# A planned attention, expert and feed-forward kernel on one core: the last slots' chain without fillers, fewer dummy transposes, one copy per half unit of y, and the carried phase row scaled by GpSimd

## The chip, the cores and the metric

The kernel runs on one core of a Trainium2 chip. The metric is the device time of one execution in microseconds (us). Three timed runs of the kernel before are at hand, and one more execution that the hardware profiler took.

## What is computed

Three stages follow each other, all in float32.

```python
# 1: gated linear recurrence, B=4, H=8, S=768, D=48
mag = np.sqrt(a_re * a_re + a_im * a_im)
scale = np.minimum(mag, 0.999) / (mag + 1e-06)
...
for t in range(S):
    new_re = ar * S_re - ai * S_im
    new_im = ar * S_im + ai * S_re
    kv = np.einsum('bhd,bhe->bhde', k[:, :, t], v[:, :, t])
    S_re, S_im = (new_re + kv, new_im)
    y[:, :, t] = np.einsum('bhd,bhde->bhe', q[:, :, t], S_re)
...
# 2: soft mixture of experts: x is y as 3072 tokens x 384; phi 384 x 32 slots
logits = x @ phi
d = softmax of logits over the tokens, c = softmax over the slots
slot_input = d.T @ x                     # 32 slots x 384
h = np.maximum(slot_input[e] @ w1[e], 0.0)   # 8 experts, 4 slots each, 384 x 1024
slot_out[e] = h @ w2[e]
x = c @ slot_out
# 3: feed-forward, 384 x 2048 x 384
h = x @ w_in
out = np.maximum(0.01 * h, h) @ w_out
```

## The kernel before, in words

The program is not written in the order in which it runs. Every step is handed to a `Plan` as an operation with an engine, a guessed cost, the tiles it reads and the tiles it writes. `emit` computes a due time for each by a pass from the end (`backward`), lets a pass from the start (`forward`) pick for each engine the next operation by earliest start and due time, repeats this six times and writes out the best order. A `lead` makes an operation due that many us earlier. An operation of VectorE (DVE) or ScalarE (ACT) that is due `FAR` us or more later than the most pressing one is a filler: it is picked only when half of its cost would fit. Tiles come from tagged pools with a fixed number of buffers (33 of the large tag `w`), and a step whose buffer is still in use waits.

**Units.** Stage 1 is cut into 12 units: 6 chunks of 128 time steps by 2 halves of the 32 sequences. A unit is a tile of 128 steps by 768 columns (16 sequences of 48). Its steps and their lines: `load_a`, `load_qkv` (L493, L352); `prep1` (L515 to L518) logarithm, exponent and ratio; `prep2` arctangent (L554), and from the third unit on the phase carried over from two units before, added into row 0 by a DMA that GpSimd (POOL) issues (L557); `phase`: running sums over the steps as a product with a triangle (PE L570), rounded by ACT (L581) and DVE (L582), absolute value (L583), and the last row times a constant for the unit after next (L586, on 32 partitions by 768); `prep3` sine and cosine (L593, L594); `decay` the sums of the logarithms and their exponents (L606, L607), whose last row goes through DRAM into a small tile (L611, L613). `prep4` multiplies q and k with them (L623, L632). `attend` is the unit's TensorE (PE) work: transposes (L647, copied by L653 and L651), scores (L662, masked by L665), y (L688), state update (L703, L713 to L716); `mE` copies y out (L724), transposes it (L728), and copies it out again in two pieces of 192 columns (L732).

Unit 0 is cut into pieces of 192, 192 and 384 columns, so that the chain at the start is short. `warm` (L823) issues transposes of the identity that compute nothing, 150 at the start and 20 after the last logits.

**Slots.** After each second unit `slots` takes the logits of 512 tokens (L748), a running maximum (L752, L754, L755), the exponent (L756), transposes (L762, L763), the slots' sums (L771, accumulated by L777) and the denominator (L778, L779). After the last chunk a product with ones brings the four groups to one maximum (L899 to L904); `si_t` adds the groups up (L911, copied by L914).

**Experts.** 64 slabs of weights of 384 KB come in over the whole program, by the queue of SyncE (SP), as buffers come free. `layer1(gr)` (L932, ReLU by ACT L937 and DVE L939, transposes L943, copies L950) and `layer2(gr)` (L968, L975, L979, L987) each run for two groups of experts. `combine` is the softmax over the slots, its transposes are L880.

**Feed-forward.** `product` multiplies the experts' output with w_in (L1005, L1008, L1009) and spreads the result (L1013, L1014, copied by L1018 and L1020). `ffn1` (L1030, then L1032 to L1034) and `ffn2` (L1047 to L1049) run over 16 chunks of the inner dimension for 8 groups of 384 tokens. w_in and w_out arrive as 64-bit words and are narrowed by `conv_wi` and `conv_wo` (L445 on ACT, L446 to L449 on DVE, and for w_out L477 and L478). These conversions are the fillers.

## Time and profile before

| | us |
|---|---|
| three timed runs | 514.16, 513.96, 512.84 (median 513.96) |
| the profiled execution | 512.59 |
| its span | 510.7 |
| PE busy | 491.8 (96%) |
| ACT busy | 357.4 (70%) |
| DVE busy | 330.4 (65%) |
| POOL busy | 13.0 (3%) |
| DMA moved | 66.98 MB |

The shares are means over stages that differ. The units run from the start to about 245, the last slots to 251, the experts and the product to 284, the feed-forward to the end. A busy PE is one with matmuls in flight, not one at its peak. In the rows "<-" behind an idle time names what ended it.

### The profile page before, as it was taken

The numbers are of one execution on the slowest core, as the hardware profiler recorded it, in microseconds if no ns is written. First come the engines' busy times: TensorE is split into PE (matmuls) and PEld (weight loads), VectorE is DVE, ScalarE is ACT, GpSimd is POOL, SyncE is SP. The second block draws the span as 40 slices with busy tenths as digits, with TensorE's granted clock in tenths as the row PEclk, the third lists the DMA queues.
The fourth block names the chain that finished last, engine by engine and source line by source line (L and its number), as shares of the span: only waits on it lengthen the run. The fifth ranks groups of instructions, "written<-read, shape, count | busy, mean of one in ns | idle before, by whom it ended". The sixth has DMA issues, their size and how long they took to land.

```text
span 510.7 us, 10607 instructions
## 1 busy us (share of the span) xinstructions
PE 491.8 (96%) x4155; PEld 447.9 (88%) x4155; DVE 330.4 (65%) x705; ACT 357.4 (70%) x702; POOL 13.0 (3%) x27
## 2 busy tenths in 40 slices
PE   8987989999999999999899999999999999999997
PEld 8785869888889888889654899999999999999997
DVE  3588999999999998997534999415500552035300
ACT  7799999999989999864204899249900993079502
POOL 1000000000000000001000000000000000000000
PEclk9999999999999999999999999999999999999999
DMA  7956253473443856679899321011000110010102
GB/s 261 361 193 186 73 174 130 99 206 104 154 127 126 247 171 235 195 242 335 287 361 399 104 62 32 2 37 42 15 1 0 47 48 1 1 46 2 47 0 92
DMA packets 43845, 66.98 MB, mean 131 GB/s; under 512 B 19098, under 2 KB 24970, under 8 KB 43796
## 3 DMA queue, kind: packets, MB, share of 16 engines
q1 hardware_dynamic: 43476, 66.29, 39.2%
q8 instruction: 32, 0.52, 0.4%
q0 software_dynamic: 320, 0.03, 0.1%
q14 instruction: 17, 0.14, 0.1%
HBM read 61.53 MB, written 4.75 MB: 130 GB/s over the span
## 4 chain that ended last, share of the span: by engine, by line
PE 68%; DVE 17%; ACT 8%; DMA 3%; issue 2%; POOL 0%; SPq 0%; POOLq 0%; ACTq 0%; DVEq 0%
PE b L1047 13%; PE b L1048 13%; PE b L1049 13%; PE b L1030 4%; PE bm L823 4%; PE bm L688 3%; PE bsc L662 3%; PE btr L647 3%; DVE sc L665 2%; PE b L932 2%; PE b L968 2%; DVE k L632 2%; DVE q L632 2%; PE bsc L703 2%; PE bc L570 2%
## 5 line engine op out<-in xcount | busy, mean ns | idle before, releaser
L1034 DVE TENSOR_TENSOR w<-x,w 128x384 fp32r<-128x384 f32 x128 | 67.8, 555 | 105.9 <-ACT w L1033 105.9
L1047 PE MATMUL b<-w 128*128 128x384 f32 x384 | 128.6, 335 | 0.8 <-ACT x L1032 0.8
L1048 PE MATMUL b<-w 128*128 128x384 f32 x384 | 128.6, 335 | 0.0
L1049 PE MATMUL b<-w 128*128 128x384 f32 x384 | 128.3, 334 | 0.0
L1047 PEld LDWEIGHTS b<-w 128*128 128x128 f32 x384 | 72.1, 188 | 1.0 <-ACT x L1032 1.0
L1049 PEld LDWEIGHTS b<-w 128*128 128x128 f32 x384 | 72.1, 188 | 0.0
L1048 PEld LDWEIGHTS b<-w 128*128 128x128 f32 x384 | 72.1, 188 | 0.0
L1056 ACT ACTIVATE k<-b 128x384 f32<-128x384 f32 x24 | 11.3, 487 | 82.5 <-PE b L1049 82.3
L1033 ACT ACTIVATE w<-x 128x384 fp32r<-128x384 f32 x128 | 62.9, 531 | 6.1 <-PE b L1049 5.0
L1032 ACT ACTIVATE x<-b 128x384 f32<-128x384 f32 x128 | 58.7, 494 | 3.8 <-PE b L1030 3.1
L662 PE MATMUL bsc<-qt,kt 96*128 96x128 f32 x384 | 51.8, 280 | 1.9 <-DVE S L715 0.8
L662 PEld LDWEIGHTS bsc<-qt,kt 96*128 96x128 f32 x384 | 46.2, 191 | 5.4 <-issue 1.9
L688 PE MATMUL bm<-sc,w 128*64 128x128 f32 (+1 forms) x384 | 36.4, 277 | 0.1
L665 DVE TENSOR_TENSOR sc<-bsc,tri_r 128x512 f32<-128x512 f32 x48 | 32.5, 682 | 3.1 <-PE bsc L662 2.9
L647 PE MATMUL btr<-ident,q 128*96 128x128 f32 x192 | 29.5, 276 | 3.8 <-ACT qt L653 2.3
L186 ACT ACT_TABLE_LOAD x25 | 32.1, 1283 | 1.2 <-PEq L1141 0.8
L703 PEld LDWEIGHTS bsc<-w,k 128*96 128x96 f32 x320 | 29.0, 165 | 3.4 <-DVE sc L665 2.5
L703 PE MATMUL bsc<-w,k 128*96 128x48 f32 x320 | 30.3, 247 | 1.6 <-DVE sc L665 1.5
L688 PE MATMUL bm<-qt,S 96*48 96x128 f32 x320 | 31.2, 272 | 0.0
L653 ACT ACTIVATE qt<-btr 96x512 f32<-96x512 f32 x48 | 28.2, 589 | 3.6 <-PE btr L647 3.5
L647 PE MATMUL btr<-ident,k 128*96 128x128 f32 x192 | 29.0, 274 | 1.3 <-ACT w L525 0.7
L647 PEld LDWEIGHTS btr<-ident,q 128*96 128x96 f32 x192 | 20.8, 127 | 8.4 <-ACT qt L653 3.3
(177 smaller groups left out, 822.8 us busy)
## 6 DMA issues: line engine op xcount, KB each, us to landing
w<-in_w_dram SPq DMA_DIRECT2D x49, 384.0 KB, 6.5
w<-in_qkv_dram SPq DMA_DIRECT2D x36, 384.0 KB, 6.0
w<-in_a_dram SPq DMA_DIRECT2D x22, 384.0 KB, 4.5
w<-in_wi_dram SPq DMA_DIRECT2D x16, 384.0 KB, 4.7
w<-in_wo_dram SPq DMA_DIRECT2D x16, 384.0 KB, 5.6
out_dram<-k SPq DMA_DIRECT2D x24, 192.0 KB, 1.9
cs<-in_w_dram SPq DMA_DIRECT2D x6, 384.0 KB, 5.0
k<-in_w_dram SPq DMA_DIRECT2D x6, 192.0 KB, 6.2
```

Of the source, the lines that this page charges most:

```text
L186: self.preload(TABLES[name])
L647: T.transpose(b()[:96, P * i:P * i + P], src()[:, i].rearrange("p t d -> p (t d)"), ident)
L662: T.matmul(b()[:, P * i:P * i + P], lhsT=k()[:96, i, :], rhs=q()[:96, i, :], start=True, stop=True)
L665: dve(c_dve(512), lambda: V.tensor_tensor(t(), b().rearrange("p (i t) -> p i t", t=P), tri.unsqueeze(1).to_broadcast([P, 4, P]), op=ALU.mu ...
L688: T.matmul(y()[64 * j:64 * j + m, o:o + P], lhsT=l, rhs=r, start=kind == 0, stop=kind == 1 or c == 0)
L703: T.matmul(b()[:96, D * i:D * i + D], lhsT=ks[i // 4]()[:, i % 4].rearrange("p t d -> p (t d)"), rhs=v()[:, D * g:D * g + D], start=True, ...
L1032: act(NG, lambda: A.activation(u(), b()[:, :NG], AF.Prelu, alpha=0.01), [b], [u])
L1033: act(NG, lambda: A.activation(g()[:, 0], u(), AF.Copy), [u], [(g, 0)])
L1034: dve(c_dve(NG), lambda: V.tensor_tensor(g()[:, 1], u(), g()[:, 0].bitcast(F32), op=ALU.subtract), [u, (g, 0)], [(g, 1)])
L1047: T.matmul(b()[:, :DM], lhsT=lh, rhs=wh()[:, i], start=f == FO[0], stop=False)
L1048: T.matmul(b()[:, :DM], lhsT=ll, rhs=wh()[:, i], start=False, stop=False)
L1049: T.matmul(b()[:, :DM], lhsT=lh, rhs=wl()[:, i], start=False, stop=f == FO[-1])
```

## The change

In words, with the lines of the changed kernel where they are new:

- The real and imaginary parts of unit 0 are loaded by two queues, SP's and ACT's; phi is loaded later, in the place of unit 0 in the plan.
- 100 dummy transposes at the start in place of 150, 14 in place of 20 at the end; their guessed cost is 0.16 in place of 0.11.
- In `phase` the rounded phase stays in the tile `im` (L582, L583); the last row is no longer scaled by DVE. It is written to DRAM (L589), read back as a tile of 128 x 6 (L590), scaled by POOL (L591) and written to DRAM again (L592), from where POOL's accumulating DMA takes it (L558).
- In `mE` one copy of 384 columns (L737) takes the place of the two.
- In `slots` the running minimum of the negated maximum is kept, so that one DVE operation goes; the exponent's own accumulator gives the row sum, so that the reduction goes. The accumulation of the last chunk is cut in three, and so is `si_t`.
- `FAR` is 10 in place of 20. The last chunk's slots, `si_t`, the end of `layer2(1)`, `product`, the first `conv_wo` and the first `ffn1` get leads of 25 or 26. `select` waits for the slots' sums.

```diff
-NEAR, FAR = 0.03, 20.0
+NEAR, FAR = 0.03, 10.0
...
-    SY.dma_start(phi, r_in)
...
+                far = u == 0 and i
+                plan.add("ACT" if far else "SP", 0.1, lambda b=b, i=i, o=o, e=e, far=far: (A if far else SY).dma_start(b()[:, o:e], a_in[u, i][:, o:e]), [], [(b, o)], nbytes=P * (e - o) * 4)
...
-            plan.add("POOL", 1.0, lambda: GP.dma_start(im()[0:1, :], cr()[127:128, :], accum_op=ALU.add), [cr], [(im, o) for o, _ in cuts(u)], nbytes=3072)
+            plan.add("POOL", 1.0, lambda: GP.dma_start(im()[0:1, :], cr().unsqueeze(0), accum_op=ALU.add), [cr], [(im, o) for o, _ in cuts(u)], nbytes=3072)
...
-            cr = s["cr"] = t_w()
-            dve(c_dve2(W), lambda: V.tensor_scalar(cr()[96:128], cs()[96:128, 1], -TWO_PI, None, op0=ALU.mult), [(cs, 1, o) for o, _ in cu], [cr])
+            row = t_dr()
+            cr = t_cr()
+            carried = s["cr"] = t_dr()
+            plan.add("SP", 0, lambda: SY.dma_start(row().unsqueeze(0), im()[P - 1:P, :]), [(im, o) for o, _ in cu], [row], nbytes=3072)
+            plan.add("SP", 0, lambda: SY.dma_start(cr(), row().rearrange("(p f) -> p f", p=P)), [row], [cr], nbytes=3072)
+            pool(0.12, lambda: GP.tensor_scalar(cr(), cr(), -TWO_PI, 0.0, op0=ALU.mult, op1=ALU.add), [], [cr])
+            plan.add("SP", 0, lambda: SY.dma_start(carried().rearrange("(p f) -> p f", p=P), cr()), [cr], [carried], nbytes=3072)
...
-        for j in range(2):
-            act(192, lambda j=j: A.activation(
-                x().rearrange("p (r j e) -> p r j e", j=2, e=D)[:, :, j, :],
-                b()[:, 0:448].rearrange("p (r w) -> p r w", w=112)[:, :, 64 * j:64 * j + D], AF.Copy), [b], [(x, j)])
+        act(384, lambda: A.activation(
+            x().rearrange("p (r j e) -> p r j e", j=2, e=D),
+            b()[:, 0:512].rearrange("p (r w) -> p r w", w=128)[:, :, 0:2 * 64].rearrange("p r (j w) -> p r j w", w=64)[:, :, :, 0:D], AF.Copy), [b], [(x, 0), (x, 1)])
...
+        plan.lead = 25.0 if last else 0.0
...
-            dve(0.07, lambda: V.tensor_tensor(m1, m1, m0, op=ALU.max), [("mx", c)], [("mx", c + 1)])
-        dve(0.07, lambda: V.tensor_scalar(n1, m1, -1.0, None, op0=ALU.mult), [("mx", c + 1)], [("nm", c + 1)])
+            dve(0.07, lambda: V.tensor_scalar(n1, m1, -1.0, n0, op0=ALU.mult, op1=ALU.min), [("mx", c + 1), ("nm", c)], [("nm", c + 1)])
...
-            dve(0.2, lambda: V.tensor_reduce(sm1(), e(), axis=AX.X, op=ALU.add), [e], [sm])
...
-    warm(150, b_m)
+    warm(100, b_m)
...
-    warm(20, b_c, [phi_mm])
+    warm(14, b_c, [phi_mm])
...
+    plan.lead = 25.0
     product()
     for f in FO[:4]:
+        plan.lead = 26.0 if f in FO[:1] else 0.0
         conv_wo(f)
```

The order changes in many places. Three of them follow. The first is PE's order at the start, up to the first transposes of unit 0: L570 (L571 after) are the sums for the decay (`tri_r`) and for the phase (`tri_p`), L823 (L832 after) the dummies. Before:

```order
L823 MATMUL bm<-ident 128x128 x78
L570 MATMUL bsc<-w,tri_r 128x192 x6
L823 MATMUL bm<-ident 128x128 x8
L570 MATMUL bm<-w,tri_r 128x384 x3
L823 MATMUL bm<-ident 128x128 x49
L570 MATMUL btr<-w,tri_p 128x192 x2
```

and after:

```order
L832 MATMUL bm<-ident 128x128 x53
L571 MATMUL bsc<-w,tri_r 128x192 x3
L832 MATMUL bm<-ident 128x128
L571 MATMUL bsc<-w,tri_r 128x192 x3
L832 MATMUL bm<-ident 128x128 x5
L571 MATMUL bm<-w,tri_r 128x384 x3
L832 MATMUL bm<-ident 128x128 x34
L571 MATMUL btr<-w,tri_p 128x192 x2
```

Ahead of the decay stand 53 dummies where 78 stood, and between decay and phase 34 where 49 stood.

The second is DVE's order around the last chunk's maximum (L752, L758 after), up to the product with the identity that the common maximum starts with (L899, L910 after). L876 (L887 after) belongs to the softmax over the slots, L800 and L804 (L809 and L813 after) to `select`. Before:

```order
L876 TENSOR_TENSOR kt<-logits,kt 128x3x64
L804 CAST sc<-stk 32x2x32
L800 TENSOR_SCALAR sc<-stk 128x512
L804 CAST sc<-stk 32x2x32
L752 TENSOR_REDUCE mx<-bsc 128x1
L804 CAST sc<-stk 32x2x32
L754 TENSOR_TENSOR mx<-mx 128x1
L804 CAST sc<-stk 32x2x32
L755 TENSOR_SCALAR nm<-mx 128x1
L804 CAST sc<-stk 32x2x32
L899 TENSOR_SCALAR kt<-ident,mx 128x128
```

and after:

```order
L887 TENSOR_TENSOR kt<-logits,kt 128x3x64 x3
L758 TENSOR_REDUCE mx<-bsc 128x1
L760 TENSOR_SCALAR nm<-mx,nm 128x1
L769 COPY dd<-bsc 128x128
L910 TENSOR_SCALAR kt<-ident,nm 128x128
```

`select` has moved behind the chain (it follows L923).

The third is SP's queue at the experts' last slabs. Before:

```order
L352 DMA qt<-in_w_dram 128x384 x2
L352 DMA x<-in_w_dram 128x384 x3
L352 DMA w<-in_w_dram 128x768 x16
L352 DMA w<-in_wo_dram 128x768 x16
L1057 DMA out_dram<-k 128x384 x24
```

and after:

```order
L352 DMA x<-in_w_dram 128x384 x2
L352 DMA w<-in_w_dram 128x768 x4
L352 DMA w<-in_wo_dram 128x768
L352 DMA w<-in_w_dram 128x768 x12
L352 DMA w<-in_wo_dram 128x768 x15
L1070 DMA out_dram<-k 128x384 x24
```

One load of w_out stands in the middle of the slabs. Its conversion stands between the two ReLUs of `layer1(1)`'s group on both engines: on ACT L445 ahead of the second L947, on DVE L446 to L449 ahead of the second L949 (L937 and L939 before).

## Rows read from the trace of the kernel before

**Rows 1.** Stages: us, busy PE, PEld, DVE, ACT, POOL, granted clock, DMA share, GB/s.
```profile
0.00:20.00 20.00, 18.57 (x151) 18.37 (x152) 7.91 (x25) 14.14 (x32) 1.61 (x9) 1.00 0.87 312
20.00:40.00 20.00, 17.22 (x158) 14.87 (x155) 15.54 (x29) 18.65 (x30) 0.93 (x1) 1.00 0.60 209
40.00:140.00 100.00, 92.35 (x923) 78.78 (x918) 98.92 (x182) 97.46 (x156) 5.09 (x6) 1.00 0.49 144
140.00:230.00 90.00, 89.85 (x1017) 79.99 (x1017) 87.39 (x177) 79.97 (x140) 2.39 (x3) 1.00 0.61 191
150.00:250.00 100.00, 98.54 (x1111) 87.39 (x1110) 92.80 (x198) 80.28 (x145) 4.67 (x9) 1.00 0.69 229
251.00:284.00 33.00, 31.52 (x415) 17.74 (x416) 14.08 (x57) 10.17 (x23) 0.70 (x2) 1.00 0.89 331
284.00:300.00 16.00, 15.36 (x86) 14.78 (x87) 15.80 (x40) 13.79 (x33) 0.00 (x0) 1.00 0.26 75
300.00:500.00 200.00, 200.00 (x1155) 199.50 (x1154) 75.40 (x155) 111.45 (x265) 0.00 (x0) 1.00 0.07 23
```

**Rows 2.** Timeline of the start, SP's queue and ACT: start us, us, what [idle before].
```profile
0.81 0.39 SPq L397 DMA_DIRECT2D phi<-in_r_dram  x1
...
3.62 0.36 ACT L515 ACTIVATE w<-w 128x192 f32<-128x192 f32 x1 [1.54 <-DMA w<-in_a_dram]
...
19.29 0.74 ACT L581 ACTIVATE cs<-btr,b_rnd 128x192 f32<-128x192 f32 x2 [1.95 <-PE btr L570]
...
22.45 0.37 ACT L593 ACTIVATE cs<-cs 128x192 f32<-128x192 f32 x1 [1.21 <-DVE w L586]
```

**Rows 3.** Timeline of the start, DVE.
```profile
7.66 0.56 DVE L517 TENSOR_TENSOR w<-w 128x384 f32<-128x384 f32 x1 [1.68 <-DMA w<-in_a_dram]
```

**Rows 4.** Timeline of the start, PE.
```profile
1.43 10.08 PE L823 MATMUL bm<-ident 128*128 128x128 f32 x78 [1.43 <-POOL ident masks.py:199]
...
13.41 5.51 PE L823 MATMUL bm<-ident 128*128 128x128 f32 x49
18.76 0.82 PE L570 MATMUL btr<-w,tri_p 128*128 128x192 f32 x4
...
29.29 0.64 PE L647 MATMUL btr<-ident,q 128*96 128x128 f32 x4 [1.33 <-ACT qt L653]
```

**Rows 5.** Groups by line and shape, DVE: busy us, mean ns, idle before.
```profile
L586 DVE TENSOR_SCALAR w<-cs 32x768 f32<-32x768 f32 x10 | 5.6, 556 | 0.2
```

**Rows 6.** Groups by line and shape, ACT.
```profile
L732 ACT ACTIVATE x<-bm 128x192 f32<-128x192 f32 x48 | 13.9, 330 | 2.0 <-PE bm L728 2.0
...
L883 ACT ACTIVATE q<-btr 128x384 fp32r<-128x384 f32 x5 | 2.3, 505 | 0.0
```

**Rows 7.** Timeline of the last slots, PE.
```profile
242.79 1.08 PE L748 MATMUL bsc<-yt,phi 112*32 112x128 f32 x32
...
250.99 5.39 PE L932 MATMUL b<-w,dd 128*32 128x256 f32 x96
```

**Rows 8.** Timeline of the last slots, DVE.
```profile
244.92 0.27 DVE L752 TENSOR_REDUCE mx<-bsc 128x1 f32<-128x128 f32 x1
...
246.26 0.28 DVE L899 TENSOR_SCALAR kt<-ident,mx 128x128 f32<-128x128 f32 x1
```

**Rows 9.** The experts: SP's loads from 250 on, their time to landing, PE's transposes.
```profile
252.47 13.41 SPq L352 DMA_DIRECT2D w<-in_w_dram  x16
...
DMA to landing us min/median/max: 3.2/7.7/8.2
...
263.18 0.64 PE L943 MATMUL b<-ident,kt 128*128 128x128 f32 x4
```

**Rows 10.** From the experts' last matmul to the feed-forward, PE.
```profile
274.93 0.55 PE L979 MATMUL b<-ident,x 128*128 128x128 f32 x3
...
283.84 0.44 PE L1047 MATMUL b<-w 128*128 128x384 f32 x1 [0.76 <-ACT x L1032]
```

**Rows 11.** Waits of SP's queue: line, for what, us in total, times, longest.
```profile
SPq L611 <- ACT w L606: 60.4, 7, 12.8
...
SPq L613 <- DMA dr<-w: 10.3, 9, 3.6
```

More of the change, by code (lines that the diff above doesn't have):

```diff
@@ L389, in tile_kernel @@
     sbuf = [sst([96, W]), sst([96, W])]
[L390 removed]
+    t_dr = Tag(dram, "dr", [W], 8)
+    t_cr = Tag(mem, "cr", [P, W // P], 2)
     b_tr = Tag(psa, "btr", [P, 512], 2)
@@ L773, in slots @@
         pe(0.9, ms, [dd] + [k for x in xs for k in ((x, 0), (x, 1))], [b3])
-        sm = t_sm()
-        sm1 = lambda: sm()[:, 0:1]
         if c:
-            dve(c_dve(384), lambda: V.scalar_tensor_tensor(acc, acc, al(), b3()[:, :DM], op0=ALU.mult, op1=ALU.add), [b3, al], ["acc"])
-            dve(0.2, lambda: V.tensor_reduce(sm1(), e(), axis=AX.X, op=ALU.add), [e], [sm])
+            for k in range(3 if last else 1):
+                x = slice(P * k, P * k + P) if last else slice(0, DM)
+                dve(c_dve(x.stop - x.start), lambda x=x: V.scalar_tensor_tensor(acc[:, x], acc[:, x], al(), b3()[:, x], op0=ALU.mult, op1=ALU.add), [b3, al], [("acc", k)] if last else [("acc", j) for j in range(3)])
             dve(0.1, lambda: V.scalar_tensor_tensor(den, den, al(), sm1(), op0=ALU.mult, op1=ALU.add), [sm, al], ["den"])
         else:
-            dve(c_dve(384), lambda: V.tensor_copy(acc, b3()[:, :DM]), [b3], ["acc"])
-            dve(0.2, lambda: V.tensor_reduce(den, e(), axis=AX.X, op=ALU.add), [e], ["den"])
+            dve(c_dve(384), lambda: V.tensor_copy(acc, b3()[:, :DM]), [b3], [("acc", j) for j in range(3)])
+        plan.lead = 0.0
     def attend(u):
@@ L822, in warm @@
         for _ in range(n):
-            pe(0.11, lambda: T.transpose(b()[:, :P], ident, ident), [], [b], after=after)
-    warm(150, b_m)
+            pe(0.16, lambda: T.transpose(b()[:, :P], ident, ident), [], [b], after=after)
+    warm(100, b_m)
     run("a0 a1 q0 P0 M0 X0 l0 P1 D0 A0 F0 A1 S0 a2")
@@ L831, in tile_kernel @@
             plan.add("SP", 0, lambda: SY.dma_start(stk, stk_in), [], ["stk"], nbytes=65536)
+        if n == 0:
+            plan.add("SP", 0, lambda: SY.dma_start(phi, r_in), [], ["phi"], nbytes=57344)
         run("a3 q1 F0 A1 S0 D0", n)
@@ L871, in combine_t @@
         for j in range(j0, j1):
-            c4, b, t = t_kt([P, 3, 4, NSL], F32R), bank(), slice(3 * j, 3 * j + 3)
+            c4, b, t = (t_k if 4 <= j < 6 else t_kt)([P, 3, 4, NSL], F32R), bank(), slice(3 * j, 3 * j + 3)
             ct = cT[j] = (t_q, t_yt)[j // 5]([P, NG], F32R)
@@ L905, in tile_kernel @@
     plan.lead = 0.0
-    warm(20, b_c, [phi_mm])
+    warm(14, b_c, [phi_mm])
     b1, b0 = b_m(), bank()
-    def si_t():
-        for k in range(3):
-            T.matmul(b1()[:, NSL * k:NSL * k + NSL], lhsT=acc[:, P * k:P * k + P], rhs=wb()[:, 0, :], start=True, stop=True)
-    pe(1.2, si_t, ["acc", wb], [b1])
-    si = dve(0.17, lambda: V.tensor_copy(siT().rearrange("p k s -> p (k s)"), b1()[:, :3 * NSL]), [b1], [siT])
+    plan.lead = 25.0
+    for k in range(3):
+        pe(0.25, lambda k=k: T.matmul(b1()[:, NSL * k:NSL * k + NSL], lhsT=acc[:, P * k:P * k + P], rhs=wb()[:, 0, :], start=True, stop=True), [("acc", k), wb], [(b1, k)])
+    si = dve(0.17, lambda: V.tensor_copy(siT().rearrange("p k s -> p (k s)"), b1()[:, :3 * NSL]), [(b1, k) for k in range(3)], [siT])
+    plan.lead = 0.0
     pe(0.3, lambda: T.matmul(b0()[:, 0:1], lhsT=wb().rearrange("p i s -> p (i s)"), rhs=den, start=True, stop=True), ["den", wb], [b0])
```

39 lines of the change are left out of this document (23 added, 16 removed).

## The prediction

> **What bounds the kernel now.** I read the busy time by stage first, then the timeline of the places where the change cuts, then the groups by line for the prices.
>
> The stages [rows 1] show four regimes. From 0 to 20 no engine but PE is full, and PE is full of dummies: DVE works 7.91 of 20 us, ACT 14.14. This is a latency chain, one short operation after another on the pieces of unit 0. From 40 to 140 DVE works 98.92 and ACT 97.46 of 100 us, and PE 92.35: three engines in balance, with DVE and ACT in front, and PE idle for 7.65. From 140 to 230 PE works 89.85 of 90 and the others have gaps: here PE is the bound, since the later chunks have the product with the state as well. From 251 to 284 the experts and the product run, PE 31.52 of 33 with the DMA at a share of 0.89. From 300 to 500 PE works 200.00 of 200. The last regime is 45% of the time, and no edit touches the number of its matmuls. So a gain must come from the start, the units, the 7 us of the last slots and the passage into the feed-forward, and each is priced from its own stage.
>
> The sum is made against the profiled execution, 512.59, which is 1.37 under the median of the three runs, 513.96. About 0.3% or 1.5 us is what a measurement of this kernel can tell from no change, so "faster" begins at 512.4.
>
> **The start: 3.8 us.** Four waits of the chain are touched.
>
> - Phi's load is the first in SP's queue, at 0.81 for 0.39, and ACT waits 1.54 for its first piece, until 3.62 [rows 2]. Phi moves away, so that the piece is issued some 0.45 earlier. But ACT now issues three loads ahead of its table load, about 0.4 each by phi's row, and can't start much before 3.4. I count 0.2.
> - DVE waits 1.68 for the last imaginary piece, until 7.66 [rows 3], which was sixth in SP's queue. On a queue of its own it is third, and issued before 2. That wait goes, but what is late next is ACT's exponent of the same piece, right in front; I count 1.1.
> - ACT waits 1.95 for the first phase sums, until 19.29 [rows 2]. PE ran them at 18.76, straight behind 49 dummies that began at 13.41 and took 5.51, while the data were ready [rows 4]. Now 34 stand there, and ahead of the decay 53 in place of 78, which took 10.08 [rows 4]. At 10.08/78 = 0.13 each, PE is 3 us earlier at the decay and 2 us more at the phase, and the wait of 1.95 falls to what the sums themselves take. I count 1.6.
> - ACT's first sine waits 1.21 for DVE, in whose queue the scaling of the last row (L586) stands [rows 2]. It is gone; I count 0.9 of the 1.21, since the absolute values stay.
>
> That makes 3.8. The ends: 1.5, if the phase sums become late for another reason, and 5.3, which is 0.45 and all three waits in full. It carries on, because ACT and DVE are hardly idle from 40 on: what they begin earlier they end earlier.
>
> **The units: 1.6 us.** DVE loses ten scalings of 0.556 [rows 5], 5.6 us, and some small operations of the slots. ACT loses 48 copies of 192 columns at 0.330 and gains 24 of 384; the nearest row is a copy of 384 from the same kind of bank, 0.505 [rows 6], so 24 x (0.660 - 0.505) = 3.7. Both savings spread over all units. About half of them fall into 40 to 140, where DVE and ACT are the bound; after 140 PE is, and they are worth nothing. In the first part DVE saves 3 and ACT 1.9, and the smaller of the two decides: 1.9. I take 1.6, as the number of table loads is the same. The ends are 0 (the order by due times finds no use for it) and 7.65, all of PE's idle time there [rows 1].
>
> POOL's new work, ten small operations on 128 x 6, and the three DMAs per unit are costed at nothing. POOL works 5.09 of 100 us [rows 1], and the carried row is needed two units later, some 30 us. SP's queue has to issue them in order; it waits 60.4 us in all for the decay's last row anyway [rows 11]. What it costs if that cover is gone is the first rival.
>
> **The last slots: 1.6 us.** The chain begins when PE ends the logits, at 242.79 + 1.08 = 243.87, and ends when layer 1 starts, at 250.99 [rows 7]. DVE takes the maximum at 244.92, 1.05 later, because operations of `select` and of the softmax over slots are in front, and reaches the product with the identity at 246.26, another 1.34 later, with three casts and the second maximum in between [rows 8]. With the order printed above, the maximum can follow the logits by a hand-over of some 0.15, which gives 0.9, and from there to the product stand a reduction of 0.27 and two short operations, some 0.65, which gives 0.7. Further down, the accumulation in three pieces costs about what it lets PE begin earlier; I count nothing. `select` is late next: it moves to a time when DVE works 14.08 of 33 us [rows 1], which covers it. The ends are 0.5 and 3. Of the six dummies fewer nothing lies on the path.
>
> **One load of w_out among the slabs: -0.8 us.** SP issues the last 16 slabs in 13.41 us from 252.47 on, and loads of this stretch land 3.2 to 8.2 after their issue, at the median 7.7 [rows 9]. In fifth place the load is issued at 252.47 + 4 x 0.84 = 255.8 and lands between 259 and 264. ACT and DVE hold the second group's ReLUs behind its conversion, and PE wants their result at 263.18 [rows 9]. With a landing at the median plus two operations of ACT, some 1.2, PE is 1.6 late; at the minimum, not at all. I take the middle, 0.8, and keep 0 to 2.5 as ends. The slabs behind it land one slab's time later too, but they are late only if PE isn't.
>
> **Into the feed-forward: 1.0 us.** From the transposes behind the experts' last matmul, 274.93, to the first matmul of the feed-forward, 283.84, PE needs 8.9 [rows 10], the last 0.76 of it a wait for ACT. Half of the transposes move ahead of the last slab's matmuls, the copies of the product are no longer mixed with conversions, and the first `ffn1` comes after four of the eight spreading pairs in place of six. I take 1.0 of the 8.9, about the wait of 0.76 and a transpose; ends 0 and 2.5. Beyond 284 DVE is full for a while, 15.80 of 16 [rows 1], so more can't be had there.
>
> **Sum:** 3.8 + 1.6 + 1.6 - 0.8 + 1.0 = 7.2, or 512.59 - 7.2 = 505.4 against the profiled execution and 506.8 against the median. The forecast lies between: **506.0**, by itself 503 to 509.
>
> **Rivals.**
>
> *SP's queue is held up by the carried row (slower).* Each unit's row goes out, comes back and goes out again by SP, which waits twice for a landing, with loads of q, k, v and slabs queued behind. The nearest row is the wait for the decay's row: 10.3 over 9, so 1.14 each, at worst 3.6 [rows 11]. Two such waits and POOL's step cost 2.7 per unit at the mean and 7.6 at worst. The cover is 60.4 over ten units, 6 each. At the mean it is hidden; at worst 1.6 per unit is not, and over ten units the time is 505.4 + 16 = 521. It decides from 6 us per unit on. For it: DMA runs at 0.87 in the first 20 us, where small transfers stand in line. Against it: after that the share is 0.49 [rows 1]. Chance 0.05.
>
> *Slabs bound the experts.* If the weights come no earlier than now, the experts end where they ended, and start, units and slots are lost up to some 2 us that PE's part gives back: 509 to 511.5. For it: a share of 0.89 from 251 on. Against: 0.69 from 150 to 250 [rows 1], and slabs wait for buffers, which come free earlier with everything else. Chance 0.12.
>
> *PE's gaps close.* If the order with `FAR` at 10 removes most of the 7.65 idle us, 4 more are won: 499.5 to 503. For it: DVE sheds 3 us there. Against: ACT sheds less. Chance 0.15.
>
> *The clock falls.* The dummies keep PE busy at the start. The granted clock is 1.00, the level of 2.4 GHz, in every stage, also from 20 to 40, where PE works 17.22 of 20 [rows 1] and an idle time of 1.33 stands in its timeline [rows 4]. If the thinner dummies let it fall to 1.2 GHz until 30, the 4 us or so of PE's work on the path would double: 505.4 + 4, about 509.5. The Trainium skill, "TensorE: Matmul & The Clock Gate", Part 1, says that half rate is the default and comes back after idling; by that rule this is where the change would hurt. The trace before shows no fall to hold against it. Chance 0.05.
>
> *Nothing to see.* The waits at the start are replaced by others, and the rest is below 1.5: 512.4 to 515. Chance 0.05.
>
> **How the numbers follow.** The forecast has the remaining 0.58. Faster are forecast, closed gaps, slabs and clock: 0.90. Same is the fifth, 0.05; slower the first, 0.05. The range leaves out the outer half of the closed gaps (0.07), the top of the slabs' case, the fifth and the first: 500.5 to 511.0.
>
> **What would show it.** In the profile after, the first phase copy of ACT (L582) should stand near 16 in place of 19.29, and the first product of unit 0 some 4 us earlier; from 40 to 140 PE's work should rise over 92.35. From the end of the logits to layer 1 it should be 5.5 in place of 7.1. A wait of ACT's L445 or PE's L953 should show the load of w_out. The feed-forward should keep the 226.9 us from its first matmul, 283.84, to the end of the span, 510.7. I am wrong if SP's waits for the carried row grow to several us, if ACT's idle time at the start stays, or if the clock leaves 1.00.

## The result, and the profile after

The changed kernel takes **506.29 us** at the median of four runs (505.94 to 507.30) against 513.40 for the kernel before (512.52 to 514.16): a ratio of 0.9864, with a 95% interval of 0.9852 to 0.9876. The forecast was 506.0. The profiled execution takes 506.31 in place of 512.59, so 6.28 are to be found in its rows.

A sum can be right with wrong terms. I follow the same instruction through both timelines and note how much earlier it comes:

| place | before | after | earlier by | won since the row above | forecast |
|---|---|---|---|---|---|
| first product of unit 0 (DVE) | 23.19 | 20.06 | 3.13 | 3.13 | 3.8 |
| last logits (PE) | 242.79 | 238.91 | 3.88 | 0.75 | 1.6 |
| layer 1 (PE) | 250.99 | 246.12 | 4.87 | 0.99 | 1.6 |
| second ReLU's transposes (PE) | 263.18 | 258.32 | 4.86 | 0.0 | -0.8 |
| product (PE) | 276.74 | 273.38 | 3.36 | **-1.50** | in the next row |
| first feed-forward matmul (PE) | 283.84 | 279.20 | 4.64 | 1.28 | 1.0 |
| last matmul (PE) | 506.97 | 500.70 | 6.27 | **1.63** | 0 |

Two steps that the prediction did not have, one of either sign, nearly cancel: that the sum came out so near is in part luck. The place of 506.0 is too. Against the profiled execution the prediction said 505.4, and 506.31 came; 506.0 was put between that and the median's 506.8.

The stages of the kernel after; columns as in [rows 1]:

```profile
0.00:20.00 20.00, 16.83 (x116) 16.04 (x117) 9.44 (x30) 16.10 (x37) 1.60 (x9) 1.00 0.90 333
...
40.00:140.00 100.00, 95.58 (x982) 83.72 (x981) 96.32 (x179) 96.97 (x150) 6.73 (x12) 1.00 0.51 137
140.00:230.00 90.00, 88.94 (x986) 78.27 (x985) 86.81 (x170) 78.32 (x128) 3.91 (x7) 1.00 0.72 229
...
284.00:300.00 16.00, 16.00 (x94) 16.00 (x94) 15.90 (x38) 16.00 (x41) 0.00 (x0) 1.00 0.18 50
```

From 40 to 140 PE works 3.2 us more than before, but from 140 to 230 it works 0.9 less. From 284 to 300 its gaps (15.36 of 16 before) are gone: ACT works 16.00 where it worked 13.79.

The start, timelines of ACT and PE; these rows answer to [rows 2, 4]:

```profile
6.24 0.52 ACT L516 ACTIVATE w<-w 128x384 f32<-128x384 f32 x1 [1.07 <-DMA w<-in_a_dram]
...
17.21 0.74 ACT L582 ACTIVATE w<-btr,b_rnd 128x192 f32<-128x192 f32 x2
...
19.05 0.36 ACT L599 ACTIVATE cs<-w 128x192 f32<-128x192 f32 x1
```

```profile
11.89 3.87 PE L832 MATMUL bm<-ident 128*128 128x128 f32 x34
16.61 0.89 PE L571 MATMUL btr<-w,tri_p 128*128 128x192 f32 x4 [0.85 <-ACT w L555]
```

The phase sums now wait 0.85 for their data and no longer stand behind dummies. ACT has a new wait: 1.07 for the last *real* piece.

The last slots, PE and then DVE; these rows answer to [rows 7, 8]:

```profile
238.91 1.08 PE L754 MATMUL bsc<-yt,phi 112*32 112x128 f32 x32
...
241.41 0.33 PE L771 MATMUL bsc<-ident,dd 128*128 128x128 f32 x1 [0.23 <-ACT dd L765]
241.57 0.40 PE L911 MATMUL bsc<-kt,ones 128*128 128x128 f32 x2
...
243.87 0.92 PE L922 MATMUL bm<-kt,acc 128*128 128x32 f32 x6
244.62 1.40 PE L832 MATMUL bc<-ident 128*128 128x128 f32 x11
246.12 2.15 PE L942 MATMUL b<-w,dd 128*32 128x256 f32 x36
```

```profile
240.06 0.29 DVE L758 TENSOR_REDUCE mx<-bsc 128x1 f32<-128x128 f32 x1 [0.58 <-PE bsc L754]
...
240.71 0.28 DVE L910 TENSOR_SCALAR kt<-ident,nm 128x128 f32<-128x128 f32 x1
...
244.82 0.26 DVE L923 COPY dd<-bm 128x96 f32<-128x96 f32 x1 [0.50 <-PE bm L922]
```

DVE's maximum follows the logits (end 239.99) by 0.07, and the operand of the product with ones follows the maximum by 0.65, as forecast. But DVE has handed the slots' input over at 245.08, and layer 1 starts at 246.12, right behind eleven dummies.

The experts, timelines of SP, ACT and PE; these rows answer to [rows 9, 10]:

```profile
249.46 0.38 SPq L352 DMA_DIRECT2D w<-in_wo_dram  x1
...
256.94 0.57 ACT L445 ACTIVATE w<-w 128x384 f32<-128x384 f32 x1 [5.96 <-DMA w<-in_wo_dram]
257.42 0.58 ACT L947 ACTIVATE kt<-b 128x512 f32<-128x512 f32 x1
```

```profile
258.32 0.64 PE L953 MATMUL b<-ident,kt 128*128 128x128 f32 x4
...
269.54 0.55 PE L990 MATMUL b<-ident,x 128*128 128x128 f32 x3 [0.70 <-ACT x L986]
270.02 1.50 PE L978 MATMUL b<-w,h 128*32 128x384 f32 x16
...
272.25 0.55 PE L990 MATMUL b<-ident,x 128*128 128x128 f32 x3 [0.73 <-ACT x L986]
273.38 2.80 PE L1018 MATMUL b<-wi,so 128*32 128x256 f32 x48 [0.59 <-DVE so L998]
...
279.20 0.45 PE L1060 MATMUL b<-w 128*128 128x384 f32 x1
```

The w_out load lands 7.5 us after its issue and ACT waits 5.96 for it, yet the ReLU behind it is in time: PE takes L953 without a wait. PE waits twice for ACT at the moved transposes instead.

### The profile page after: what moved, and what is told of

Read it like the earlier page. It is cut to its first block, busy times and chain, and to the rows that moved or that the text cites. A ratio compares the mean times of both kernels' runs of the same rounds, so it can differ in the third digit from the quotient of the medians.

```text
span 504.6 us, 10532 instructions
## 1 busy us (share of the span) xinstructions
PE 486.0 (96%) x4099; PEld 443.4 (88%) x4099; DVE 325.7 (65%) x686; ACT 359.4 (71%) x684; POOL 17.1 (3%) x37
## 4 chain that ended last, share of the span: by engine, by line
PE 75%; DVE 10%; ACT 9%; DMA 4%; issue 1%; SPq 0%; POOL 0%; ACTq 0%; POOLq 0%
PE b L1060 13%; PE b L1062 13%; PE b L1061 13%; PE bm L694 6%; PE bsc L668 5%; PE b L1043 4%; PE btr L653 4%; PE bsc L709 3%; PE bc L571 3%; PE b L978 2%; PE b L942 2%; DVE w L629 2%; DMA w<-in_a_dram 2%; ACT L186 2%; DVE q L638 1%; DVE k L638 1%
## 5 line engine op out<-in xcount | busy, mean ns | idle before, releaser
L1047 DVE TENSOR_TENSOR w<-x,w 128x384 fp32r<-128x384 f32 x128 | 68.9, 556 | 104.3 <-ACT w L1046 103.5
L1045 ACT ACTIVATE x<-b 128x384 f32<-128x384 f32 x128 | 59.9, 489 | 3.0 <-PE b L1043 2.3
L653 PEld LDWEIGHTS btr<-ident,k 128*96 128x96 f32 x192 | 20.8, 128 | 7.3 <-ACT qt L659 3.3
```

Source lines behind the costliest of these rows:

```text
L653: T.transpose(b()[:96, P * i:P * i + P], src()[:, i].rearrange("p t d -> p (t d)"), ident)
L1045: act(NG, lambda: A.activation(u(), b()[:, :NG], AF.Prelu, alpha=0.01), [b], [u])
L1047: dve(c_dve(NG), lambda: V.tensor_tensor(g()[:, 1], u(), g()[:, 0].bitcast(F32), op=ALU.subtract), [u, (g, 0)], [(g, 1)])
```

## The experiments

Each undoes or changes one part of the changed kernel. Times are medians; ratios are against the kernel before on the same chip. The changed kernel's 506.29 and 0.9864 are what they compare with; since intervals are about 0.0015 either way (0.8 us), each reading leans on its timeline too.

**More dummies again**

```diff
-            pe(0.16, lambda: T.transpose(b()[:, :P], ident, ident), [], [b], after=after)
+            pe(0.11, lambda: T.transpose(b()[:, :P], ident, ident), [], [b], after=after)
...
-    warm(100, b_m)
+    warm(150, b_m)
...
-    warm(14, b_c, [phi_mm])
+    warm(20, b_c, [phi_mm])
```

> The changed kernel with 150 and 20 dummy transposes (guessed cost 0.11) again; the order of ACT and SP stays word for word, DVE's but for two products swapped, PE's but for the dummies. Theory: the thinner dummies are the larger part of the gain at the start. PE then reaches the first phase sums near 18.6 in place of 16.61, ACT's first phase copy moves from 17.21 to about 19.2, and the 2.0 us are carried to the end: 508.3 against 506.3. Rival A: the loads on a second queue made the start shorter and the dummies only fill time in which the data are not there: at most 0.3 us, 506.6. Rival B: the delay is real at the start but is swallowed by slack in the units: the phase copy at 19.2, the end within 0.7 us of 506.3.

Measured: 509.85, ratio 0.9935 [0.9920, 0.9949]. The start and the slots, PE:

```profile
13.56 5.51 PE L832 MATMUL bm<-ident 128*128 128x128 f32 x49
18.91 0.82 PE L571 MATMUL btr<-w,tri_p 128*128 128x192 f32 x4
...
246.39 1.95 PE L832 MATMUL bc<-ident 128*128 128x128 f32 x16
```

The phase copy comes at 19.44, 2.2 later; 1.7 of it is left at the last logits (240.57), and the longer row of dummies ahead of layer 1 adds 0.55. So rivals A and B fall, and the theory holds for the start. The timed loss is larger than the profiled execution's 2.4 us; its excess over that I can't place (the mean granted clock is 0.999 or 1.00 in all six executions).

**The loads on one queue again**

```diff
+    SY.dma_start(phi, r_in)
     make_identity(nc, ident)
...
-                far = u == 0 and i
+                far = False
...
-        if n == 0:
-            plan.add("SP", 0, lambda: SY.dma_start(phi, r_in), [], ["phi"], nbytes=57344)
```

> The changed kernel with the imaginary parts of unit 0 and phi loaded by SP's queue again, phi first; the orders of PE and DVE stay as they are, ACT loses its three load issues. Theory: the load part of the prediction (1.3 us) was worth about 0.2 only, since the wait for the imaginary piece was replaced by one for the real piece. ACT's first logarithm comes at 3.6 to 3.7 in place of 3.50, DVE's operation on the last piece near 7.6 in place of 7.46, the first phase copy at most 0.4 later than 17.21: 506.4 to 506.8. Rival: the two queues are worth what was forecast, 1.3 us: the first phase copy near 18.5 and 507.6.

Measured: 507.44, ratio 0.9879 [0.9861, 0.9896], which overlaps with the changed kernel's. In the timeline DVE's operation on the last piece comes at 7.40 (7.46 with two queues) and the phase copy at 17.15 (17.21). One execution each would not tell this, since these loads land with a scatter of 1.5 us (last section): in the twelve profiles with two queues that operation begins between 7.14 and 8.66, at the median 7.40, and with one queue it is 7.40 here and 7.66 in the kernel before. So the rival's 1.3 us falls; the second queue is worth 0.3 at most. The higher median is not the loads': three of the four executions show a mean granted clock of 0.993 to 0.997, and the one at 1.00 takes 506.25.

**The row scaled by DVE again**

```diff
-            pool(0.12, lambda: GP.tensor_scalar(cr(), cr(), -TWO_PI, 0.0, op0=ALU.mult, op1=ALU.add), [], [cr])
...
+            cr = s["cr"] = t_w()
+            dve(c_dve2(W), lambda: V.tensor_scalar(cr()[96:128], im()[96:128], -TWO_PI, None, op0=ALU.mult), [(im, o) for o, _ in cu], [cr])
```

> The changed kernel with the carried phase row scaled by DVE again, on 32 partitions by 768, and handed to GpSimd's accumulating load directly; the rounded phase stays where the change put it. The planner's order moves in many places with it. Theory: the scaling stands ahead of ACT's first sine again, which then follows the phase copy by 2.9 to 3.2 us in place of 1.84, and DVE has 0.556 us more per unit: the last logits 1.0 to 2.0 us later than 238.91, the time 507.3 to 508.3. Rival A: the trips of the row through DRAM and GpSimd cost as much as they save: within 0.4 us of 506.3. Rival B: only the start counts and its gain is lost in the units: the sine later by 1.2, the last logits by less than 0.4.

Measured: 509.68, ratio 0.9926 [0.9913, 0.9940]. The first sine stays early, at 18.84, and the scaling stands behind it; the first product is at 19.85, the last logits at 242.52. All of the loss is in the units: 222.67 us from first product to last logits in place of 218.85. Not all of it is the scaling's: the granted clock fell in the units of this execution (last section), and it did in three of the six (mean clock 0.997), at 510.14 to 510.62. The other three take 508.69 to 509.22, 2.6 more at the median than the changed kernel's three at the full clock (505.94 to 506.31). One place, PE and DVE:

```profile
47.68 1.54 PE L570 MATMUL bc<-w,tri_r 128*128 128x512 f32 x6 [2.02 <-DVE w L582]
```

```profile
46.69 0.94 DVE L582 SCALAR_TENSOR_TENSOR w<-w,bc 128x768 f32<-128x768 f32 x1
47.55 0.68 DVE L665 TENSOR_TENSOR sc<-bsc,tri_r 128x512 f32<-128x512 f32 x1
48.15 0.55 DVE L583 TENSOR_SCALAR cs<-w 128x768 int32<-128x768 int32 x1
48.73 0.56 DVE L586 TENSOR_SCALAR w<-w 32x768 f32<-32x768 f32 x1
```

DVE works without a gap and PE waits for it. So the theory's place was half wrong (nothing at the start) and its size too small (3.4 us by the medians, 2.6 at the full clock); both rivals fall.

**Two y copies again**

```diff
-        act(384, lambda: A.activation(
+        for j in range(2):
+            act(192, lambda j=j: A.activation(
```

> The changed kernel with two copies of 192 columns of y per half unit in place of one of 384; the columns' distance in the bank stays as changed. The planner's order moves in many places with it. Two copies took 0.660 in the kernel before and one takes 0.48 now, so ACT works 24 x 0.18 = 4.3 us more. Theory: the units' part of the gain is small, as ACT bounds them only up to 140: the last logits 0.3 to 0.9 us later, 506.6 to 507.2. Rival A: half of it counts, as the prediction has it: 1.9 to 2.1 us, 508.2 to 508.4. Rival B: nothing counts, since DVE and PE bound the units: within 0.3 us of 506.3.

Measured: 507.24, ratio 0.9886 [0.9873, 0.9899]. In the profiled execution the last real piece of unit 0 happened to land late (ACT waits 2.28 for it; DVE's operation on the last imaginary piece begins at 8.66, elsewhere at 7.14 to 8.10), and the first product is at 21.26. From there to the last logits it takes 218.84, where the changed kernel takes 218.85. That looks like rival B, but two differences cancel in it. PE's phase sums of unit 2 and its last logits, here:

```profile
39.15 1.56 PE L571 MATMUL bc<-w,tri_p 128*128 128x512 f32 x4 [1.34 <-ACT w L613]
...
240.10 1.08 PE L755 MATMUL bsc<-yt,phi 112*32 112x128 f32 x32
```

The changed kernel begins these sums at 39.54, because it waits there for the carried row (see the rivals below), which here has landed at 38.4. So the late start is made up at unit 2; from there to the last logits it takes 200.95 in place of 199.37. About 0.4 of this 1.6 are four transposes that PE does behind the place here and ahead of it there (an estimate from their distance of 0.38 to 0.44 in the rows); the kernels with nine rounds and with a large buffer, whose orders moved too, take 199.28 and 198.74. So the two copies cost the units some 1.2 us in these rows (one execution each, and 0.6 of chance between those orders), which fits the loss of the median, 0.95. Rival B falls; between the theory (up to 0.9) and rival A (1.9 to 2.1) it lies in the middle.

**Nine planner's rounds (control)**

```diff
-ROUNDS = 6
+ROUNDS = 9
```

> A control: the changed kernel with nine planner's rounds in place of six, so the same operations in another order, by nobody's intention. It says how much of a difference of a kernel whose order has moved everywhere is the order's chance. Theory: the last logits move by less than 0.7 us and the time by less than 1: then effects of the carried row and of the copies above 1 us can be read. Rival: the order's chance is worth 1 to 3 us, and the 3.3 us of the start and 0.6 us of the units can't be told apart by such kernels.

Measured: 505.55, ratio 0.9849 [0.9836, 0.9862]; units 217.59. The order alone is worth 0.8 us of time and 1.3 us in the units, so the theory's bound of 0.7 there was too tight. Most of it is one place, PE's phase sums of unit 2:

```profile
38.05 1.56 PE L571 MATMUL bc<-w,tri_p 128*128 128x512 f32 x4
```

The changed kernel begins them at 39.54 after a wait for the carried row; here the row has landed at 37.6, and there is no wait. Of the 1.49 us 0.32 were there at the first product, so 1.17 of the 1.3 are won here. The loss with DVE's scaling stands out of the order's chance, a smaller one would not.

**No leads at the slots**

```diff
-        plan.lead = 25.0 if last else 0.0
+        plan.lead = 0.0
...
-            dve(0.35, lambda sl=sl: V.tensor_scalar(sl(), stk.unsqueeze(1).to_broadcast([P, 4, P]), 0.0, None, op0=ALU.mult), ["stk"], [sl], after=[si])
+            dve(0.35, lambda sl=sl: V.tensor_scalar(sl(), stk.unsqueeze(1).to_broadcast([P, 4, P]), 0.0, None, op0=ALU.mult), ["stk"], [sl])
...
-    plan.lead = 25.0
+    plan.lead = 0.0
     for k in range(3):
```

> The changed kernel without the leads on the last chunk's slots and on the slots' sums, and with select free to run before them; DVE's casts of select then stand in the chain again, the small operations that the change removed stay removed. Theory: the leads make most of the shorter way from the logits to layer 1, 6.1 in place of 7.1 us: the maximum comes 0.7 to 1.0 us later behind the logits, and the time is 507.0 to 507.3. Rival: the way is shorter because of the removed operations (the second maximum and the row sum): the leads are worth at most 0.3, 506.3 to 506.6.

Measured: 507.00, ratio 0.9873 [0.9856, 0.9890]. The last logits start at 239.41, DVE's maximum at 241.29 and layer 1 at 247.59. From the logits' end (1.08 after their start) to layer 1 that is 7.1 us again, as in the kernel before, although the removed operations stay removed. The slots' sums start at 245.77, 5.28 after the logits' end (5.62 before, 3.88 in the changed kernel), so the operations by themselves gain 0.34 there. The dummies ahead of layer 1, seven in place of five before, take it back. The theory holds for the stage: of the 1.74 at the slots' sums the order makes 1.40. The medians are too close to show it.

**No leads at the product and the feed-forward**

```diff
-    plan.lead = 25.0
+    plan.lead = 0.0
     product()
...
-        plan.lead = 26.0 if f in FO[:1] else 0.0
+        plan.lead = 0.0
...
-        plan.lead = 25.0
+        plan.lead = 0.0
         for j in range(2):
```

> The changed kernel without the leads on the product, the first conversion of w_out and the first chunks of the feed-forward. In its order the six transposes stand behind the last product of the experts again, and the load of w_out has left the place among the slabs; on DVE and ACT the product's copies are mixed with conversions again. Theory: three things add up. The transposes give back 1.2 us, the load of w_out nothing (no engine that PE waits for was late by it), and from the product's first matmul to the feed-forward's first it takes 7.1 us again in place of 5.8, which costs 1.3: 506.1 to 506.7, with the product 1.2 earlier and the feed-forward's start where it is. Rival A: the load of w_out cost the 0.8 of the prediction: PE's second transposes to layer 1's output 0.8 earlier, 505.3 to 505.8. Rival B: the leads of the product are worth nothing: the feed-forward begins 1.2 earlier, 505.1.

Measured: 507.78, ratio 0.9889 [0.9874, 0.9904], slower than all three said. The product does come 1.0 earlier (272.37), and the feed-forward starts 6.3 later, at 278.68. But from its first to its last matmul it then takes 223.96 (278.68 to 502.64) in place of 221.50. The stage, and PE's waits from 278 to 305 (us in total, times, longest):

```profile
284.00:300.00 16.00, 14.61 (x80) 13.43 (x80) 15.77 (x39) 13.88 (x31) 0.00 (x0) 1.00 0.29 77
```

```profile
PE b L1043 <- ACT x L1045: 1.2, 2, 0.6
PE b L1060 <- ACT x L1045: 0.3, 1, 0.3
```

So most of the leads' gain lies behind the first feed-forward matmul: 0.5 us ahead of it (6.31 from the product to there, 5.82 with the leads) and 2.5 behind it, where the first activations are no longer mixed with conversions and PE does not wait for them.

**The first group's transposes at the end again**

```diff
-        pe(0.33, tr, [so], [b2])
+        pe(0.33, tr, [so], [b2], after=[last])
```

where `last` is the last product of the second group.

> The changed kernel with one more wait: the transposes of the first expert group's output come after the last product of the second group, so that PE has no gap ahead of them and the two sets of three stand behind each other, as in the kernel before. Theory: the transposes between the slabs' products cost the changed kernel the waits of 0.70 and 0.73 for ACT, of which about 0.25 remains in the old order: 1.2 us less, 505.1. Rival A: the waits are only moved on, since DVE's copies and ACT's conversions behind them come later: the first feed-forward matmul stays within 0.4 us of 279.20, 506.0 to 506.5. Rival B: the reordered first chunks of the feed-forward cost more than that: above 506.6.

Measured: 505.23, ratio 0.9840 [0.9825, 0.9855].

```profile
270.28 0.55 PE L993 MATMUL b<-ident,x 128*128 128x128 f32 x3
271.02 0.55 PE L993 MATMUL b<-ident,x 128*128 128x128 f32 x3 [0.19 <-ACT x L989]
272.15 2.80 PE L1021 MATMUL b<-wi,so 128*32 128x256 f32 x48 [0.58 <-DVE so L1001]
...
277.96 0.34 PE L1063 MATMUL b<-w 128*128 128x384 f32 x1
```

The product and the feed-forward begin 1.2 us earlier. Of this 0.2 was there at layer 1 (245.91 in place of 246.12), so 1.0 is the transposes': the theory holds, and that it holds to a tenth is luck. The two waits of 0.70 and 0.73 have become one of 0.19.

**Three dummies in place of 14 behind the logits**

```diff
-    warm(14, b_c, [phi_mm])
+    warm(3, b_c, [phi_mm])
```

> The changed kernel with 3 dummies in place of 14 behind the last logits; nothing else moves on any engine: the 11 dummies between the slots' sums and layer 1 are gone. Theory: they hold layer 1 up. PE ends them at 246.02 and starts layer 1 at 246.12, while DVE has handed over the slots' input at 245.08; without them layer 1 starts some 0.9 us earlier, near 245.2, and the time is 505.4. Rival A: layer 1 waits for the slabs as much as for the dummies: within 0.3 us of 506.3. Rival B: PE's idle time before layer 1 lets the granted clock fall from 1.00, and the first products of layer 1 run longer: 507 or more.

Measured: 505.31, ratio 0.9846 [0.9832, 0.9859].

```profile
245.06 0.91 PE L922 MATMUL bm<-kt,acc 128*128 128x32 f32 x6
246.37 1.93 PE L942 MATMUL b<-w,dd 128*32 128x256 f32 x32 [0.40 <-issue]
```

From the slots' sums to layer 1 it takes 1.31 in place of 2.25, and the granted clock is 1.00 there. The theory holds.

**The row's tile in a large buffer**

```diff
-            cr = t_cr()
+            cr = s["crw"] = t_w([P, W // P])
...
-            plan.add("SP", 0, lambda: SY.dma_start(carried().rearrange("(p f) -> p f", p=P), cr()), [cr], [carried], nbytes=3072)
...
+            cr, crw = st[u - 2]["cr"], st[u - 2]["crw"]
+            plan.add("SP", 0, lambda: SY.dma_start(cr().rearrange("(p f) -> p f", p=P), crw()), [crw], [cr], nbytes=3072)
```

> The changed kernel with the small tile of the carried row in a buffer of the large tag w, written to DRAM only ahead of its use two units later: GpSimd still scales it, DVE does not, but a large buffer is held per unit about as long as in the kernel before. PE's, DVE's and ACT's orders stay almost as they are. Theory: the carried row's part of the gain is DVE's time, 0.556 us per unit on an engine that is full from 40 to 140: the last logits stay within 0.7 us of 238.91 and the time within 0.8 of 506.3. Rival: it is the large buffers that come free earlier, and with them the loads and the tiles of the next units: then this kernel loses most of the 3.4 us that the kernel with DVE's scaling lost, 508.5 to 509.7, with longer waits of SP's queue for w tiles.

Measured: 506.21, ratio 0.9871 [0.9853, 0.9890]; units 217.88. It looks like the theory, but it is a weak test. A wait of SP's queue (us in total, times, longest):

```profile
SPq L558 <- POOL w L592: 23.4, 10, 3.6
```

SP stood waiting at this write each of the ten times and issued it right behind GpSimd, so the buffer was held for a short while and not for some 30 us. What it shows is that a short use of a large buffer costs nothing. Whether DVE's time or a long-held buffer makes the loss with DVE's scaling was not settled. For DVE's time speaks that in the kernel with DVE's scaling neither PE nor DVE waits for a load from 20 to 235.

**FAR at 20 again**

```diff
-NEAR, FAR = 0.03, 10.0
+NEAR, FAR = 0.03, 20.0
```

> The changed kernel with FAR at 20 again, so that conversions are fillers only if due 20 us or more later than the most pressing operation. The order moves in many places. Theory: FAR is worth no more than the order's chance (the control with nine rounds moved the time by 0.8): 505.5 to 507.1, and PE's work from 40 to 140 stays at 95 or more. Rival: FAR at 10 is what closes PE's gaps in the units: PE's work from 40 to 140 falls back to 92 to 94 and the time is 507.5 to 509.

Measured: 505.88, ratio 0.9854 [0.9841, 0.9868]; PE works 95.89 from 40 to 140. FAR is worth nothing that stands out of the order's chance, and it is not what closed PE's gaps.

**The three together: a better version**

The edits are the late transposes, the three dummies and the nine rounds from above.

> The changed kernel with the transposes of the first group's output behind the last product of the experts, 3 dummies in place of 14 behind the last logits, and nine planner's rounds. Theory: the three add up, since they touch different places: 1.2 for the transposes, 0.9 for the dummies and 0.8 for the order, 503.4 against 506.3. Rival A: the slabs' loads bound the experts once they begin earlier: 504.2 to 505. Rival B: the order's 0.8 was chance and does not come again with the other two: 504.2.

Measured: **502.96**, ratio 0.9797 [0.9784, 0.9810]: faster than both kernels, and the three gains add up (503.4 expected). Layer 1 and the feed-forward, PE:

```profile
243.66 0.64 PE L942 MATMUL b<-w,dd 128*32 128x256 f32 x8 [0.40 <-issue]
...
276.44 0.34 PE L1063 MATMUL b<-w 128*128 128x384 f32 x1
```

The profiled execution, 503.79, is one of the two longest of the five, and its stages add up less well: the order wins 1.5 up to the last logits and the dummies 0.9 at layer 1, but from layer 1 to the feed-forward it takes 32.78, where the kernel with the late transposes takes 32.05 and the changed kernel 33.08. PE's products of the last slab begin at 266.20 and take 2.72 in place of 1.50. That is rival A's mechanism beginning to show; that the slab's load is what they wait for, the rows don't name.

## Why the prediction was right, and where its steps were not

**The start, 3.8 forecast, 3.13 found.** The step that failed is "That wait goes ... I count 1.1" for the imaginary piece. DVE takes its last piece at 7.46 in place of 7.66. I had named ACT's exponent of the same piece as late next; ahead of that stands the real piece, for which ACT now waits 1.07. With the loads undone the phase copy stays where it is: two queues did not bring the last piece sooner than one by more than 0.3. The dummies were worth 2.1 to 2.2 at the phase sums where I counted 1.6. The first sine follows the phase copy by 1.84 in place of 3.16, so 1.3 where I counted 0.9. But the kernel with DVE's scaling has the 1.84 too, so it is not the scaling's absence that won it. In the kernel before the sine wrote over the part of `cs` that the scaling read, so it had to come behind the scaling, which needs all three pieces. The change leaves the rounded phase in `im`, and in both kernels the sine waits for the scaling no longer. Of the 3.40 won at the sine 0.27 is lost at the first product, which now stands in DVE's queue behind the last piece's absolute value. ACT's first logarithm is 0.12 earlier, near the 0.2.

**The units, 1.6 forecast, 0.75 found.** The savings came, and a term that was put at nothing took part of them back. I split the stage at the phase sums of unit 2 (41.36 before, 39.54 after). From there to the last logits the changed kernel takes 199.37 in place of 201.43, so 2.06 are won; without the four transposes that have moved ahead of the place it is some 1.6, the forecast. But from the first product to there it takes 19.48 in place of 18.17, so 1.31 are lost. The step that failed is that POOL's new work and the three DMAs per unit "are costed at nothing": PE waits 1.28 there for the carried row (rows under the rivals). With nine rounds the row is in time, that stretch takes 18.31, and the units 217.59. "The smaller of the two" savings, ACT's 1.9, is borne out as far as the undone y copies go, which cost some 1.2 behind unit 2. The undone scaling cost more, 2.6 us at the full clock, in the changed program's order; that is not the mirror of the change, since the kernel before carried the same scaling through units only 0.75 longer (219.60). Why it costs so much more in the new order, no run tells.

**The last slots, 1.6 forecast, 0.99 found.** The two terms, 0.9 and 0.7, came: the slots' sums start 3.88 after the logits' end in place of 5.62, so 1.74 earlier. The step that failed is "Of the six dummies fewer nothing lies on the path". Once the chain is shorter, the eleven that stand ahead of layer 1 end last; taking them away gives 0.9. The undone leads showed that 1.40 of the 1.74 is the order's.

**One load of w_out, -0.8 forecast, 0 found.** The load landed 7.5 after its issue, as the median said, but it was issued 6.3 earlier than I had put it, at 249.46. The slabs ahead of it start at 247.61 in place of 252.47, and four of them took 1.75 where I put 3.4.

**Into the feed-forward, 1.0 forecast, -1.50 and +1.28 found.** I counted the moved transposes among the gains. They are a loss: their operand is a copy by ACT, 0.58 long, of the product that PE has just ended, and PE's queue cannot go on to the next slab meanwhile. Put behind the last product again, they give 1.0 back. Of the 1.28 won behind the product the undone leads account for 0.49; what made the rest, no run tells.

**The feed-forward, "more can't be had there", 1.63 found.** I read DVE's 15.80 of 16 as the bound. PE was waiting for ACT, which worked 13.79. PE's wait behind the first feed-forward matmul in the kernel before (us in total, times, longest):

```profile
PE b L1030 <- ACT x L1032: 0.6, 1, 0.6
```

The changed kernel has no wait there. So the order on ACT was what could be mended; without the leads PE falls to 14.61 of 16.

**The rivals.** A sign of being wrong that the prediction named did come: SP waits for DVE's phase row (L589) up to 8.9 us and for GpSimd's step (L592) 25.7 in all, up to 3.9. SP's queue was not held up as a whole, since its wait for the decay's row, 60.4 before, is down to 9.4. But the carried row is on the path once, at unit 2. The row of GpSimd's accumulating DMA among the issues from 19 to 40 (last number: us to landing), and what PE does then:

```profile
w<-dr POOLq DMA_DIRECT2D x1, 3.0 KB, 6.5
```

```profile
39.54 1.53 PE L571 MATMUL bc<-w,tri_p 128*128 128x512 f32 x4 [1.28 <-ACT w L516]
```

It was issued at 32.90, so it lands at 39.4; the row names ACT, whose operation had long been done (in the kernel with three dummies the same wait, 1.41, is put down to the DMA). Before, it was issued at 36.33 and landed in 2.0, ahead of these sums:

```profile
41.36 1.56 PE L570 MATMUL bc<-w,tri_p 128*128 128x512 f32 x4 [1.12 <-ACT w L607]
```

So 1.28 us is lost there in the changed kernel, and 0.6 to 1.8 in six more of the profiles. The slabs did not bound the experts of the changed kernel. PE's gaps closed by 3.2 of 7.65 from 40 to 140; the last logits gained only 0.75 in the units, since 1.31 went at unit 2, ahead of that stretch, and PE works 0.9 less from 140 to 230. The clock is in the last section.

## What to carry to other kernels

When a chain is shortened, look at what is queued on the same engine behind it, fillers and dummies too: what had cover before is the next thing on the path. A short operation that needs another engine's result should not be put between two long ones on an in-order queue, unless that result is older than the operation ahead of it. And a gain that comes from a planner's order should be tested by undoing the operation and the order apart: here the leads made 1.40 of the 1.74 us at the slots, and the removed operations alone 0.34. Where a stage's length has not moved, it is worth splitting: the undone y copies cost 1.2 us that a wait which was gone elsewhere hid.

## What the runs showed of the hardware

**The granted clock fell in the middle of the units, in some executions of the same program.** The kernel with three dummies has the changed kernel's order word for word up to the slots. Its stages by 1 us:

```profile
37.00:38.00 1.00, 0.53 (x4) 0.39 (x4) 0.96 (x2) 1.00 (x2) 0.00 (x0) 1.00 0.07 28
38.00:39.00 1.00, 0.08 (x1) 0.00 (x0) 1.00 (x2) 1.00 (x3) 0.00 (x0) 1.00 0.85 146
39.00:40.00 1.00, 0.51 (x1) 0.50 (x2) 1.00 (x3) 0.97 (x2) 0.00 (x0) 0.58 0.85 260
40.00:41.00 1.00, 1.00 (x2) 0.34 (x1) 1.00 (x3) 0.21 (x1) 0.00 (x0) 0.50 0.74 32
...
43.00:44.00 1.00, 0.55 (x5) 0.30 (x4) 0.53 (x1) 1.00 (x3) 0.00 (x0) 1.00 0.32 126
```

PE had worked little ahead of it, waiting for the carried row; the clock went to 0.50 (1.2 GHz) from about 39.2 and was at 1.00 (2.4 GHz) again by 43. The phase sums in it took 2.90, where the changed kernel took 1.53, and the last logits came at 240.10 in place of 238.91. The changed kernel's own profile, with the same gaps, shows 1.00 throughout. Four of the fourteen profiles have such a fall in the units: this one, the one with DVE's scaling (near 48.5, behind an idle time of 2.02), the one without the product's leads (near 40; its last logits are 0.4 later, 0.2 of it from the start) and the one with FAR at 20 (near 38, behind 1.67). The Trainium skill, "TensorE: Matmul & The Clock Gate", Part 1, says that the half rate comes back after idling; these rows agree, and they add that it need not come in each execution.

The mean granted clock of the timed executions tells the same without a profile. In the kernel before (30 executions, run beside the experiments) it is never under 0.999. In the changed kernel and the eleven with its 100 dummies it is 0.993 to 0.998 in 19 of 52, one of the changed kernel's four among them (507.30, the others 505.94 to 506.31), and within one kernel these executions are mostly about 1 us longer. So the change did let the clock fall, as my rival feared, but in some executions only, for 1 us and not 4, and in the profiles behind idle times in the units and not at the start. With 150 dummies none of six executions fell; six are too few to say that more dummies prevent it.

At the start the rows' clock is no proof. They give 1.00 from 0 on, but in the changed kernel PE, which ran nothing but dummies there, began 6 to 7 of them per us from 4 to 7 and 11 from 7 to 8.

**The first loads land with a scatter of 1.5 us.** In the kernels with the start unchanged, DVE's operation on the last piece of unit 0 begins between 7.14 and 8.66. Not all of it reaches the end: the kernel with the late transposes was 0.6 behind at the first product and 0.2 ahead at the last logits. Most of that is unit 2, where its wait for the carried row was 0.61 in place of 1.28.

**The carried row's DMA landed later by the new way.** GpSimd's accumulating DMA of 3 KB at unit 2 landed 4.3 to 7.0 us after its issue in the twelve profiles where it reads the row from DRAM, and after 2.0 and 3.0 in the two where it reads it from a tile. The loads in flight differ as well, so whether they or the way through DRAM make the difference stays open.
